# A gated sum of a Fourier mix and a SwiGLU layer on one core: gate applied at the spill, two Strassen sums left to DMA, w2 parts in the common buffer pool, wider x blocks

## The chip, the core and the metric

The kernel runs on one core of one Trainium2 chip. The metric is the device time of one execution in microseconds; every time given for the runs is the median of three. Engine names are those of the profile: PE is TensorE's matmul, PEld its weight load, DVE is VectorE, ACT is ScalarE, POOL is GpSimd, SP is SyncE, which here only issues DMAs. A name with a q (SPq, ACTq, POOLq) is the engine's instruction queue.

## The reference

With x of 2048 rows and 512 columns, in float32:

```python
g = sigmoid((x * gate_w).sum(-1, keepdims=True))           # one gate per row
a = Cr_seq @ (x @ Cr_hid.T) - Ci_seq @ (x @ Ci_hid.T)      # real part of a 2-D Fourier transform
b = (silu(x @ w1) * (x @ w3)) @ w2                         # F = 1376
out = g * a + (1 - g) * b
```

The Fourier matrices are inputs, 2048 x 2048 and 512 x 512, real and imaginary parts.

## The kernel before

Every product of float32 matrices is made of three matmuls: `split(hi, lo, src)` (L75) rounds `src` to the faster type on ScalarE (`hi`, L76) and takes the rest on VectorE (`lo`, L77), and `mm3` (L79) multiplies hi by hi, hi by lo and lo by hi. All matmuls therefore stand at L81, all splits at L76 and L77. On top of that the products are made in blocks of two by two by a scheme with seven products in place of eight (Strassen's in Winograd's form). It needs sums of blocks: T1 = B12 + B11, T2 = T1 + B22, T3 = B22 + B12, T4 = T2 + B21 (in the gate and up products the signs differ).

The work runs in five stages on PE. Everything is computed transposed: features on the 128 partitions, rows of x along the free axis.

1. **Gate and up, first half of x** (`gate_up(1, 11)`, product 0 being made without the scheme by `plain`). Each of 11 steps i makes 128 columns of both w1 and w3 for 1024 rows of x: `first1`, `first2` and `second`. The x blocks are loaded by `load_xo` as two tiles of 512 columns for each block, summed by `sum_xo` (L144) and split by `split_xo`. A score column for the gate g is part of the last w1 block; `put_score` brings it out. The result h(i) (128 x 1024) lies in a buffer of the pool `f4` until it is used.
2. **Down projection, first half** (`down(0)`): 11 chunks c of 24 matmuls in eight accumulators `acc`. `prep_dn` splits h(c) into `ho` (two buffers in the pool `dn`) and w2's part into `w2o` (two buffers in `dn`), and writes the split part of w2 to memory (`w2sp`). At the end b times (1 - g) is stored in `nbsp`. `gates` makes the sigmoid and stores it in `gsp`.
3. **Gate and up, second half of x** (`gate_up(11, 22)`). Beside it `prep_d` splits the Fourier matrix along D and stores it (`dsp`).
4. **Down projection, second half** (`down(1)`). The split w2 parts come back from `w2sp`, by a DMA that ScalarE issues (L260) into `w2o`. Beside it `load_a` loads x once more in another layout (xr) and makes and splits its sums (xm) into A1 and A2, and the first blocks of the sequence matrix (`cc`, tiles c) are loaded.
5. **The Fourier transform** (matmuls into P). First along the sequence: four blocks `blk` 0 to 3 of 28 steps, weights A1 and A2; then along D: blocks 4 and 5 of 14 steps, weights D1 and D2. Each step is 12 matmuls; the last two steps are made together, 24 matmuls for each half of the rows. `load_c` issues loads eight steps ahead of a step, `sum_c` makes T1, T2 and T4 on VectorE four steps ahead (L509), `split_c` splits three steps ahead into one of four `zo` buffers. T3 is made in the buffer of B22 by an accumulating DMA that GpSimd issues once B22 has been split (L520). The four results Z of a block of the sequence transform are written to `zsp` by `spill`, and the D transform loads its blocks from there. `spill` of the D transform multiplies by the gate (L561), adds b's part (L566, at the end L563) and stores the output.

The pool `f4` has 13 buffers of 128 x 1024 float32. h, x staging, w2's raw parts, xr, xm, gates, c blocks and output parts all take their buffers there, and an instruction that needs one waits until one is released.

The framework orders each engine's instructions by program order and by its own estimate of when each is ready, so an instruction can stand some steps ahead of its place in the text; each engine then works through its list in order. A DMA waits in its issuing queue, and what is behind it waits too. The order of steps and the lead of loads in the transform are written out by hand:

```python
CHAIN = (("P1", "B11"), ("P5", "T1"), ("P6", "T2"), ("P3", "B22"),
         ("P7", "T3"), ("P2", "B21"), ("P4", "T4"))
ORDER = [CHAIN] * NTB + [tuple(CHAIN[i] for i in (0, 5, 1, 2, 3, 4, 6))] * (NTB // 2)
LEAD = 3
AHEAD = 5
```

## Time and profile before

| | |
|---|---|
| three runs | 736.51, 736.87, 739.08 us; median 736.87 us |
| the profiled execution | 742.17 us, of which the span is 740.3 us |
| granted TensorE clock, mean | 0.994 |
| PE busy | 724.2 us, 98% of the span, 3145 matmuls |
| VectorE busy | 537.8 us, 73% |
| ScalarE busy | 362.4 us, 49% |
| GpSimd busy | 17.8 us, 2% |
| DMA | 128.21 MB, 173 GB/s on average |

The profile is one execution on the chip. Its stages can be told by the tiles that the matmuls write: C, X, Y and Z for gate and up, acc for the down projection, P for the Fourier transform. Matmuls are pipelined, so a busy PE is not PE at its peak: the pace (matmuls in a stretch against its length) says more. A wait is put down to the engine or DMA whose signal came last by this profile. "Granted clock" is the share of TensorE's full clock in a stretch.

### The profile page before, as it was taken

The numbers are of one execution on the slowest core, as the hardware profiler recorded it, in microseconds if no ns is written. First come the engines' busy times: TensorE is split into PE (matmuls) and PEld (weight loads), VectorE is DVE, ScalarE is ACT, GpSimd is POOL, SyncE is SP. The second block draws the span as 40 slices with busy tenths as digits, with TensorE's granted clock in tenths as the row PEclk, the third lists the DMA queues.
The fourth block names the chain that finished last, engine by engine and source line by source line (L and its number), as shares of the span: only waits on it lengthen the run. The fifth ranks groups of instructions, "written<-read, shape, count | busy, mean of one in ns | idle before, by whom it ended". The sixth has DMA issues, their size and how long they took to land.

```text
span 740.3 us, 8392 instructions
## 1 busy us (share of the span) xinstructions
PE 724.2 (98%) x3145; PEld 592.2 (80%) x3145; DVE 537.8 (73%) x681; ACT 362.4 (49%) x476; POOL 17.8 (2%) x24
## 2 busy tenths in 40 slices
PE   8999999999999999889999999999999999999996
PEld 5888878888888888778888888888888888887784
DVE  5997786584598968596857686667657675565977
ACT  5755565453466645461444445444444543453532
POOL 0000000000000000000010001000100010000000
PEclk9999999999999999999999999999999999999999
DMA  7122135835157305693767724783378329997642
GB/s 255 35 81 85 58 122 191 283 129 200 58 205 264 128 0 159 232 300 141 277 107 235 256 86 87 226 260 110 65 221 270 128 41 269 395 345 213 215 109 90
DMA packets 37324, 128.21 MB, mean 173 GB/s; under 512 B 3874, under 2 KB 4002, under 8 KB 36260
## 3 DMA queue, kind: packets, MB, share of 16 engines
q1 hardware_dynamic: 32532, 110.91, 43.1%
q0 software_dynamic: 2880, 10.49, 7.9%
q10 hardware_dynamic: 1872, 6.29, 2.6%
q8 instruction: 24, 0.39, 0.2%
q14 instruction: 16, 0.13, 0.1%
HBM read 96.73 MB, written 30.94 MB: 172 GB/s over the span
## 4 chain that ended last, share of the span: by engine, by line
PE 83%; issue 5%; DVE 5%; DMA 5%; ACT 1%; SPq 0%; ACTq 0%; POOLq 0%; POOL 0%; DVEq 0%
PE P L81 42%; PE X L81 15%; PE acc L81 13%; PE Z L81 8%; PE Y L81 4%; DMA c<-zsp 2%; PE C L81 2%; DMA xs<-xt 1%; DMA w2o<-w2sp 1%; DVE zo L77 1%; DVE xs L144 1%; DVE c L509 0%; DVE xo L77 0%; DVE ho L77 0%; DVE w2o L77 0%
## 5 line engine op out<-in xcount | busy, mean ns | idle before, releaser
L81 PE MATMUL P<-zo,a 128*128 128x512 f32 x1344 | 304.8, 389 | 0.0
L81 PEld LDWEIGHTS P<-zo,a 128*128 128x128 f32 x1344 | 252.3, 188 | 52.3
L77 DVE TENSOR_TENSOR zo<-c,zo 128x1024 fp32r<-128x1024 f32 x140 | 171.1, 1224 | 105.3 <-ACT zo L76 103.4
L76 ACT ACTIVATE zo<-c 128x1024 fp32r<-128x1024 f32 x140 | 147.6, 1059 | 177.8 <-PE P L81 142.7
L81 PE MATMUL acc<-ho,w2o 128*128 128x512 f32 x528 | 124.2, 397 | 4.2 <-DMA w2o<-w2sp 2.1
L81 PEld LDWEIGHTS acc<-ho,w2o 128*128 128x128 f32 x528 | 101.1, 192 | 27.0 <-ACT ho L76 2.5
L81 PE MATMUL X<-xo,wb 128*128 128x512 f32 x378 | 94.2, 390 | 0.2
L81 PEld LDWEIGHTS X<-xo,wb 128*128 128x128 f32 x378 | 70.6, 188 | 16.3 <-ACT u L239 0.8
L509 DVE TENSOR_TENSOR c<-c,c 128x1024 f32<-128x1024 f32 x60 | 73.3, 1224 | 10.5 <-DMA c<-cc 6.7
L81 PE MATMUL P<-zo,d 128*128 128x512 f32 x336 | 78.2, 392 | 2.6 <-DVE zo L77 1.3
L81 PEld LDWEIGHTS P<-zo,d 128*128 128x128 f32 x336 | 62.8, 188 | 17.8 <-DVE zo L77 2.6
L81 PE MATMUL X<-xo,wa 128*128 128x512 f32 x126 | 32.9, 391 | 0.0
L81 PE MATMUL Y<-xo,wa 128*128 128x512 f32 x126 | 32.3, 389 | 0.0
L81 PE MATMUL Z<-xo,wa 128*128 128x512 f32 x126 | 32.2, 389 | 0.0
L81 PE MATMUL Z<-xo,wb 128*128 128x512 f32 x126 | 32.2, 389 | 0.0
L77 DVE TENSOR_TENSOR wb<-wu,wb 128x1024 fp32r<-128x1024 f32 x21 | 25.7, 1224 | 8.5 <-ACT wb L76 8.2
L77 DVE TENSOR_TENSOR ho<-h,ho 128x1024 fp32r<-128x1024 f32 x22 | 26.9, 1221 | 6.9 <-ACT ho L76 6.9
L76 ACT ACTIVATE wa<-ws 128x768 fp32r<-128x768 f32 (+2 forms) x23 | 18.8, 816 | 25.2 <-PE Z L81 25.2
L76 ACT ACTIVATE ho<-h 128x1024 fp32r<-128x1024 f32 x22 | 23.1, 1050 | 11.2 <-PE acc L81 9.9
L520 POOL DMA_DIRECT2D c<-cc x16 | 14.1, 879 | 599.6 <-DVE zo L77 599.6
L81 PEld LDWEIGHTS X<-xo,wa 128*128 128x128 f32 x126 | 23.4, 188 | 5.4 <-DVE wa L77 0.4
L81 PEld LDWEIGHTS Z<-xo,wa 128*128 128x128 f32 x126 | 23.6, 188 | 5.0 <-ACT u L241 0.2
(92 smaller groups left out, 538.7 us busy)
## 6 DMA issues: line engine op xcount, KB each, us to landing
c<-cc SPq DMA_DIRECT2D x64, 512.0 KB, 4.4
ws<-w SPq DMA_DIRECT2D x21, 512.0 KB, 3.6
c<-cc POOLq DMA_DIRECT2D x16, 512.0 KB, 5.4
c<-zsp SPq DMA_DIRECT2D x16, 512.0 KB, 8.1
w2sp<-w2o SPq DMA_DIRECT2D x11, 512.0 KB, 2.7
w2o<-w2sp ACTq DMA_DIRECT2D x11, 512.0 KB, 4.5
nbsp<-b SPq DMA_DIRECT2D x8, 512.0 KB, 3.1
dsp<-d SPq DMA_DIRECT2D x4, 1024.0 KB, 5.7
```

Of the source, the lines that this page charges most:

```text
L76: nc.scalar.activation(hi, src, AF.Copy)
L77: nc.vector.tensor_sub(lo, src, hi.bitcast(F32))
L81: nc.tensor.matmul(ps, u, v, start=first and n == 0, stop=last and n == 2, skip_group_check=chain)
L144: nc.vector.tensor_sub(staged(g, q, k), *(staged(g, q, v) for v in SUMS[k]))
L509: nc.vector.tensor_add(t, t, RAW[blk, b, q])
L520: nc.gpsimd.dma_start(src, block(blk, 1, q), accum_op=ALU.add)
```

## The change

- **Gate.** In the sequence transform each result Z is multiplied by the gate of its columns before it is stored (two multiplications of 128 x 512 for each of 16 results; for the result of P4 these read the accumulator, in place of two ScalarE copies). The gate of a block is loaded when the block begins, into a tile of its own with two buffers. The D transform no longer multiplies; its last result is added straight from the accumulator. The two gate tiles beside D1 and D2 and their loads are gone.
- **T1 and T3 of the D transform.** Both get a buffer of their own: B12 is loaded into it and B11 or B22 is added by an accumulating DMA of GpSimd, right after the load. T1's load has its place two steps before the block's first step, T3's at its fifth step, less the lead of eight steps. T2 and T4 are still summed on VectorE, in T1's buffer. The sequence transform keeps its way.
- **w2 parts.** In the second down projection the split parts go to buffers of `f4` and are loaded by SP, two chunks ahead.
- **x blocks.** One tile of 128 x 1024 for each block and each sum in place of two of 512 wide, each in a buffer taken when it is loaded or summed; one DMA, one sum and one split for each (the first split stays in two halves). The split blocks lie in one tile. The first w block is issued ahead of the first x block, and SP issues all of them.
- **Warm-up.** 11 matmuls on zeros at the start in place of 7.

The core of the diff (the host's arrangement of x, and the same renaming in `prod`, `plain` and x1 to x3, are left out):

```diff
-WARM = 7
+WARM = 11
...
+    def load_xo(g, k):
+        if g not in XO:
+            XO[g] = xo.tile([P, 2, 7, 2, 512], F32R, tag="xo", name=f"xo{g}")
+        ST[g, k] = wide(f"xs{g}_{k}")
+        nc.sync.dma_start(ST[g, k], xt[g, XRAW.index(k)])
...
     def sum_xo(g, k):
-        for q in range(2):
-            nc.vector.tensor_sub(staged(g, q, k), *(staged(g, q, v) for v in SUMS[k]))
+        ST[g, k] = wide(f"xs{g}_{k}")
+        nc.vector.tensor_sub(ST[g, k], *(ST[g, v] for v in SUMS[k]))
...
+    def load_w2(i):
+        if NC <= i < 2 * NC:
+            W2O[i] = f4.tile([P, 2, 512], F32R, tag="f4", name=f"w2o{i}")
+            nc.sync.dma_start(W2O[i].bitcast(F32), w2sp[i - NC])
...
     def prep_dn(i):
         g, c = divmod(i, NC)
-        o = dn.tile([P, 2, 512], F32R, tag="w2o", name=f"w2o{i}")
-        if g == 1:
-            nc.scalar.dma_start(o.bitcast(F32), w2sp[c])
-        elif c % 2 == 0:
+        if g == 0 and c % 2 == 0:
...
     def down(g, extra):
...
         for c in range(NC):
+            if c == 0:
+                load_w2(g * NC + 1)
+            load_w2(g * NC + c + 2 if g == 1 else 0)
             if c + 1 < NC:
                 prep_dn(g * NC + c + 1)
...
                 if i == i1 - 2:
+                    load_w2(i1 - NC)
                     prep_dn(i1 - NC)
...
-    load_xo(0, 0, 1, (nc.sync, nc.scalar))
     load_w(0, 0, 1)
+    load_xo(0, "B11")
...
+    NEED = [(("B11", 0, 0), ("B12", 1, 1), ("B22", 2, 1), ("B21", 5, 0))] * NTB + [
+        (("B11", 0, 0), ("B21", 1, 0), ("T1", 2, 6), ("B22", 3, 1), ("T3", 5, 6))] * (NTB // 2)
...
     def split_c(m):
...
-        if form == "B22":
-            nc.gpsimd.dma_start(src, block(blk, 1, q), accum_op=ALU.add)
+        if form == "B22" and blk < NTB:
+            nc.gpsimd.dma_start(src, block(blk, "B12", q), accum_op=ALU.add)

     def load_c(m):
         while LOADS and LOADS[0][0] <= m:
             _, blk, k, q = LOADS.pop(0)
-            r = RAW[blk, BLOCKS[k], q] = wide(f"c{k}_{blk}_{q}")
-            nc.sync.dma_start(r, block(blk, k, q))
+            r = RAW[blk, k, q] = wide(f"{k}_{blk}_{q}")
+            nc.sync.dma_start(r, block(blk, "B12" if k in ("T1", "T3") else k, q))
+            if k in ("T1", "T3"):
+                nc.gpsimd.dma_start(r, block(blk, "B11" if k == "T1" else "B22", q),
+                                    accum_op=ALU.add)
...
     def spill(blk, k, t, ps=None):
-        last = blk == len(NQ) - 1 and k == 1
+        src = [t[:, r] for r in range(2)] if ps is None else ps
         if blk < NTB:
-            if ps is not None:
-                for r in range(2):
-                    nc.scalar.activation(t[:, r], ps[r], AF.Copy)
+            for r in range(2):
+                nc.vector.tensor_mul(t[:, r], src[r], GT[blk])
             return nc.sync.dma_start(z_rows(blk, k), flat(t))
-        gt, b, o = gated.pop((blk, k))
+        b, o = other.pop((blk, k))
+        if ps is None:
+            nc.vector.tensor_add(flat(t), flat(t), flat(b))
+            return nc.sync.dma_start(o, t)
         for r in range(2):
-            nc.vector.tensor_mul(t[:, r], t[:, r] if ps is None else ps[r], gt)
-            if last:
-                nc.vector.tensor_add(t[:, r], t[:, r], b[:, r])
-                (nc.scalar if r else nc.sync).dma_start(o[:, r], t[:, r])
-        if not last:
-            nc.vector.tensor_add(flat(t), flat(t), flat(b))
-            nc.sync.dma_start(o, t)
+            nc.vector.tensor_add(t[:, r], ps[r], b[:, r])
+            (nc.scalar if r else nc.sync).dma_start(o[:, r], t[:, r])
...
+    def load_gate(blk):
+        GT[blk] = ut.tile([P, 512], F32, tag="gate", name=f"gate{blk}", bufs=2)
+        nc.sync.dma_start(GT[blk], gsp[blk // 2, :, blk % 2 * 512 : (blk % 2 + 1) * 512])
...
     def step(m):
         blk, q, k, form = STEPS[m]
+        if m == START[blk] and blk < NTB:
+            load_gate(blk)
...
-    GT = [yd.tile([P, 1024], F32, tag=f"g{g}", name=f"g{g}") for g in range(2)]
...
-        elif k < 2 * KD + 2:
-            nc.sync.dma_start(GT[k - 2 * KD], gsp[k - 2 * KD])
```

More of the change, by code (lines that the diff above doesn't have):

```diff
@@ L64, in fnet_swiglu_gate_kernel @@
     dn_cm, dn = pool("dn", 2, "right")
-    xo_cm, xo = pool("xo", 2, "left")
+    xo_cm, xo = pool("xo", 1, "left")
     wo_cm, wo = pool("wo", 2, "left")
@@ L121, in fnet_swiglu_gate_kernel, with flat_x, split_xo @@
     XO, ST = {}, {}
-    def load_xo(g, t, j, queues=(nc.sync, nc.sync)):
-        if g not in ST:
-            ST[g] = [[wide(f"xs{g}_{q}_{i}") for i in range(4)] for q in range(2)]
-            XO[g] = [xo.tile([P, 2, 7, 512], F32R, tag="xo", name=f"xo{g}_{q}") for q in range(2)]
-        for q in range(2):
-            queues[q].dma_start(ST[g][q][t][:, j * 512 : (j + 1) * 512],
-                                xt[g, q, :, t * 1024 + j * 512 : t * 1024 + (j + 1) * 512])
-    AT = {"B12": (0, 0), "B11": (0, 1), "B21": (1, 0), "B22": (1, 1),
-          "T1": (2, 0), "T2": (2, 1), "T3": (3, 0), "T4": (3, 1)}
+    XRAW = ("B12", "B11", "B21", "B22")
+    def flat_x(ap):
+        return ap.rearrange("p q n -> p (q n)")
+    def load_xo(g, k):
[3 more added lines that the diff above has]
+        nc.sync.dma_start(ST[g, k], xt[g, XRAW.index(k)])
     OPS = ("B11", "B21", "B22", "T1", "T2", "T3", "T4")
     SUMS = {"T1": ("B12", "B11"), "T2": ("B22", "T1"), "T3": ("B22", "B12"), "T4": ("B21", "T2")}
-    def staged(g, q, k):
-        t, j = AT[k]
-        return ST[g][q][t][:, j * 512 : (j + 1) * 512]
     def sum_xo(g, k):
-        for q in range(2):
-            nc.vector.tensor_sub(staged(g, q, k), *(staged(g, q, v) for v in SUMS[k]))
-    def split_xo(g, *ks):
-        n = OPS.index(ks[0])
-        for q in range(2):
-            o, (t, j) = XO[g][q], AT[ks[0]]
-            split(o[:, 0, n : n + len(ks), :].rearrange("p a n -> p (a n)"),
-                  o[:, 1, n : n + len(ks), :].rearrange("p a n -> p (a n)"),
-                  ST[g][q][t][:, j * 512 : (j + len(ks)) * 512])
+        ST[g, k] = wide(f"xs{g}_{k}")
+        nc.vector.tensor_sub(ST[g, k], *(ST[g, v] for v in SUMS[k]))
+    def split_xo(g, k):
+        o = XO[g][:, :, OPS.index(k)]
+        split(flat_x(o[:, 0]), flat_x(o[:, 1]), ST[g, k])
     WS, WA, WB = {}, {}, {}
@@ L191, in prod @@
         w, wi = (WA[i], wi) if wi < 3 else (WB[i], wi - 3)
+        x = XO[g]
         for q in range(2):
             sl = slice(q * P, (q + 1) * P)
-            x = XO[g][q]
-            mm3(ps, w[:, 0, wi, sl], w[:, 1, wi, sl], x[:, 0, xi, :], x[:, 1, xi, :],
+            mm3(ps, w[:, 0, wi, sl], w[:, 1, wi, sl], x[:, 0, xi, q, :], x[:, 1, xi, q, :],
                 start and q == 0, q == 1, chain)
@@ L266, in prep_dn @@
         if g == 0:
+            o = dn.tile([P, 2, 512], F32R, tag="w2o", name=f"w2o{i}")
             split(o[:, 0], o[:, 1], W2R[g, c // 2][:, (c % 2) * 512 : (c % 2 + 1) * 512])
             nc.sync.dma_start(w2sp[c], o.bitcast(F32))
-        W2O[i] = o
+            W2O[i] = o
         t = dn.tile([P, 2, 1024], F32R, tag="ho", name=f"ho{i}")
@@ L356, in xb @@
         def xb(k):
-            return lambda q, h: XO[0][q][:, h, k, :]
+            return lambda q, h: XO[0][:, h, k, q, :]
         w21 = lambda h, sl: a21[:, h, sl]
@@ L378, in fnet_swiglu_gate_kernel @@
     load_w(0, 1, 4)
-    load_xo(0, 1, 0)
-    load_xo(0, 0, 0)
+    load_xo(0, "B21")
+    load_xo(0, "B12")
     load_w(1)
-    load_xo(0, 1, 1)
+    load_xo(0, "B22")
     load_w(2)
@@ L389, in fnet_swiglu_gate_kernel @@
     prep_wa(0, 0, 1)
-    split_xo(0, "B11")
+    for q in range(2):
+        split(XO[0][:, 0, 0, q], XO[0][:, 1, 0, q], ST[0, "B11"][:, q * 512 : (q + 1) * 512])
     next(step)
@@ L396, in fnet_swiglu_gate_kernel @@
     next(step)
-    for q in range(2):
-        sl = slice(q * 512, (q + 1) * 512)
-        split(b12[:, 0, sl], b12[:, 1, sl], staged(0, q, "B12"))
+    split(b12[:, 0], b12[:, 1], ST[0, "B12"])
     next(step)
@@ L425, in x1 @@
     def x1():
-        for t, j in ((0, 1), (1, 0), (0, 0), (1, 1)):
-            load_xo(1, t, j)
+        for k in ("B11", "B21", "B12", "B22"):
+            load_xo(1, k)
     def x2():
@@ L433, in x2 @@
         sum_xo(1, "T2")
-        split_xo(1, "T1", "T2")
+        split_xo(1, "T1")
+        split_xo(1, "T2")
     def x3():
@@ L438, in x3 @@
         sum_xo(1, "T4")
-        split_xo(1, "T3", "T4")
+        split_xo(1, "T3")
+        split_xo(1, "T4")
         split_xo(1, "B22")
@@ L481, in fnet_swiglu_gate_kernel @@
     START = [sum(NQ[:blk]) * len(CHAIN) for blk in range(len(NQ) + 1)]
-    BLOCKS = ("B11", "B12", "B22", "B21")
+    NEED = [(("B11", 0, 0), ("B12", 1, 1), ("B22", 2, 1), ("B21", 5, 0))] * NTB + [
+        (("B11", 0, 0), ("B21", 1, 0), ("T1", 2, 6), ("B22", 3, 1), ("T3", 5, 6))] * (NTB // 2)
+    PLACE = [{"T1": "B12", "T2": "B12", "T4": "B12", "T3": "B22"}] * NTB + [
+        {"T2": "T1", "T4": "T1"}] * (NTB // 2)
     LEAD = 3
@@ L488, in fnet_swiglu_gate_kernel @@
     LOADS = sorted((START[blk] + n * nq - e + q, blk, k, q)
-                   for blk, nq in enumerate(NQ) for q in range(nq)
-                   for k, n, e in (((0, 0, 0), (1, 1, 1), (2, 2, 1), (3, 5, 0)) if blk < NTB else
-                                   ((0, 0, 0), (3, 1, 0), (1, 2, 1), (2, 3, 1))))
+                   for blk, nq in enumerate(NQ) for q in range(nq) for k, n, e in NEED[blk])
     def z_rows(tb, k):
@@ L497, in block @@
         if blk < NTB:
-            return cc[blk, k, q]
-        return z_rows(2 * (blk - NTB) + (0, 1, 1, 0)[k], (0, 0, 2, 2)[k] + q)
+            return cc[blk, ("B11", "B12", "B22", "B21").index(k), q]
+        return z_rows(2 * (blk - NTB) + (k in ("B12", "B22")), 2 * (k in ("B21", "B22")) + q)
     def sum_c(m):
@@ L506, in sum_c @@
         b = {"T1": "B11", "T2": "B22", "T4": "B21"}.get(form)
-        if b:
-            t = RAW[blk, "B12", q]
+        if b and form in PLACE[blk]:
+            t = RAW[blk, PLACE[blk][form], q]
             nc.vector.tensor_add(t, t, RAW[blk, b, q])
@@ L515, in split_c @@
         blk, q, k, form = STEPS[m]
-        src = RAW[blk, {"T1": "B12", "T2": "B12", "T4": "B12", "T3": "B22"}.get(form, form), q]
+        src = RAW[blk, PLACE[blk].get(form, form), q]
         t = ZO[m] = zo.tile([P, 2, 1024], F32R, tag="zo", name=f"zo{m}")
         split(t[:, 0], t[:, 1], src)
-        if form == "B22":
-            nc.gpsimd.dma_start(src, block(blk, 1, q), accum_op=ALU.add)
+        if form == "B22" and blk < NTB:
+            nc.gpsimd.dma_start(src, block(blk, "B12", q), accum_op=ALU.add)
     def load_c(m):
@@ L551, in spill @@
     def spill(blk, k, t, ps=None):
-        last = blk == len(NQ) - 1 and k == 1
+        src = [t[:, r] for r in range(2)] if ps is None else ps
         if blk < NTB:
-            if ps is not None:
-                for r in range(2):
-                    nc.scalar.activation(t[:, r], ps[r], AF.Copy)
+            for r in range(2):
+                nc.vector.tensor_mul(t[:, r], src[r], GT[blk])
             return nc.sync.dma_start(z_rows(blk, k), flat(t))
-        gt, b, o = gated.pop((blk, k))
+        b, o = other.pop((blk, k))
+        if ps is None:
+            nc.vector.tensor_add(flat(t), flat(t), flat(b))
+            return nc.sync.dma_start(o, t)
         for r in range(2):
-            nc.vector.tensor_mul(t[:, r], t[:, r] if ps is None else ps[r], gt)
-            if last:
-                nc.vector.tensor_add(t[:, r], t[:, r], b[:, r])
-                (nc.scalar if r else nc.sync).dma_start(o[:, r], t[:, r])
-        if not last:
-            nc.vector.tensor_add(flat(t), flat(t), flat(b))
-            nc.sync.dma_start(o, t)
-    gated, LAST = {}, []
+            nc.vector.tensor_add(t[:, r], ps[r], b[:, r])
+            (nc.scalar if r else nc.sync).dma_start(o[:, r], t[:, r])
+    GT, other, LAST = {}, {}, []
+    def load_gate(blk):
+        GT[blk] = ut.tile([P, 512], F32, tag="gate", name=f"gate{blk}", bufs=2)
+        nc.sync.dma_start(GT[blk], gsp[blk // 2, :, blk % 2 * 512 : (blk % 2 + 1) * 512])
     def load_nb(blk, k):
@@ L579, in load_nb @@
         nc.sync.dma_start(b, nb)
-        gated[blk, k] = GT[tb // 2][:, tb % 2 * 512 : (tb % 2 + 1) * 512], b, o
+        other[blk, k] = b, o
     def step(m):
         blk, q, k, form = STEPS[m]
+        if m == START[blk] and blk < NTB:
+            load_gate(blk)
         if q == 0 and blk >= NTB and k in RESULT:
@@ L681 @@
     xb = [xh[:, :, 0, 1], xh[:, :, 0, 0], xh[:, :, 1, 0], xh[:, :, 1, 1]]
-    xq = x.T.reshape(2, 2, P, 2, 2, TB).transpose(3, 1, 2, 0, 4, 5)
-    xq = xq.transpose(0, 1, 3, 4, 2, 5)
+    xq = x.T.reshape(2, 2, P, 2, 2, TB).transpose(3, 0, 4, 2, 1, 5)
+    xq = [xq[:, 0, 1], xq[:, 0, 0], xq[:, 1, 0], xq[:, 1, 1]]
     w13 = np.zeros((2, D, NC * P), np.float32)
@@ L695 @@
         "xn": np.stack(xb, 2).reshape(NG, P, 2 * D),
-        "xt": np.stack([xq[:, :, 0, 1], xq[:, :, 0, 0], xq[:, :, 1, 0], xq[:, :, 1, 1]], 3)
-        .reshape(2, 2, P, 4 * TB),
+        "xt": np.stack(xq, 1).reshape(2, 4, P, 2 * TB),
         "cc": np.stack(cb, 1).reshape(NTB, 4, NG // 2, P, 2 * TB),
```

## The prediction

> **What bounds the kernel now.** I read the page first, then a table of stages, then the chain of waits, then the waits and timelines of the stages that lose time. The page:

> ```profile
> span 740.3 us, 8392 instructions
> PE 724.2 (98%) x3145; PEld 592.2 (80%) x3145; DVE 537.8 (73%) x681; ACT 362.4 (49%) x476; POOL 17.8 (2%) x24
> ```

> TensorE is the bound, and only time in which it is held up can be won. No matmul is added or removed. The chain of waits, in order of time, gives the pace and the places:

> ```profile
> 281.07 16.47 PE acc L81 x72
> 299.52 23.63 PE acc L81 x96
> 323.17 7.39 DMA w2o<-w2sp
> 330.69 18.19 PE acc L81 x72
> 348.89 310.11 PE P L81 x1368
> ```

> The last row is the pace: 310.11/1368 = 0.2267 us a matmul, with nothing lost in 310 us. The down projection of the second half (281.07 to 348.89, 67.8 us) has 264 matmuls, 59.8 us at that pace: 8.0 us are lost there. The stage table says how (columns: busy PE, PEld, DVE, ACT, POOL; granted clock; DMA share; GB/s):

> ```profile
> 176.00:281.00 105.00, 105.00 (x463) 86.27 (x462) 80.05 (x138) 58.11 (x91) 0.00 (x0) 1.00 0.39 135
> 281.00:300.00 19.00, 17.03 (x75) 13.65 (x74) 14.91 (x30) 13.77 (x22) 0.00 (x0) 1.00 0.59 192
> 300.00:324.00 24.00, 24.00 (x100) 19.66 (x99) 18.46 (x36) 11.02 (x19) 0.00 (x0) 0.93 0.82 274
> 324.00:349.00 25.00, 22.88 (x95) 18.44 (x94) 19.67 (x26) 9.98 (x15) 0.00 (x0) 0.93 0.49 165
> 349.00:450.00 101.00, 101.00 (x447) 83.67 (x446) 71.24 (x63) 46.74 (x52) 3.62 (x4) 1.00 0.60 187
> ```

> PE stands still about 2 us twice (19.00-17.03, 25.00-22.88), and after each halt the granted clock is 0.93 for some 25 us, 1.7 us lost each time: 2 x (2.1+1.7) = 7.6 of the 8.0. The timelines name the first halt:

> ```profile
> 292.03 0.33 ACTq L260 DMA_DIRECT2D w2o<-w2sp  x1
> 298.47 1.04 ACT L76 ACTIVATE ho<-h 128x1024 fp32r<-128x1024 f32 x1
> 299.50 1.94 PE L81 MATMUL acc<-ho,w2o 128*128 128x512 f32 x6 [1.97 <-ACT ho L76]
> DMA to landing us min/median/max: 3.1/4.5/7.4
> ```

> PE starts at 299.50, before the split named (298.47+1.04 = 299.51) has ended, so the name is wrong: the w2 load issued at 292.03 plus the longest landing of that tile (last line, the view of tile w2o) is 299.4. The second halt is the w2 load issued at 323.17 and landed 7.39 us later. Both were issued when a chunk (24 matmuls, 5.44 us) freed one of two buffers, so they had 5.44 us and took 7.4.

> The second transform has 336 matmuls (76.2 us) and takes from 653.4 to 734.1: 4.4 us lost, here:

> ```profile
> 681.91 0.50 PE L81 MATMUL P<-zo,d 128*128 128x512 f32 x1 [1.18 <-ACT zu L617]
> 682.69 3.07 PE L81 MATMUL P<-zo,d 128*128 128x512 f32 x12 [0.28 <-DVE zo L77]
> 686.53 36.02 PE L81 MATMUL P<-zo,d 128*128 128x512 f32 x156 [0.76 <-DVE zo L77]
> 722.83 11.29 PE L81 MATMUL P<-zo,d 128*128 128x512 f32 x47 [0.28 <-DVE zo L77]
> ```

> These are T3's steps (the 11th and 12th of 14 in each block, so 27 us after 653.4 and again). T3's sum is an accumulating DMA on GpSimd's queue, issued only after B22 was split:

> ```profile
> 670.43 0.86 POOL L520 DMA_DIRECT2D c<-zsp  x1 [56.29 <-DVE zo L77]
> 673.84 0.86 POOL L520 DMA_DIRECT2D c<-zsp  x1 [2.55 <-DMA c<-zsp]
> ```

> Last, the tail. The last matmul ends at 734.12, then VectorE still multiplies by the gate and adds, and the store goes out:

> ```profile
> 735.73 0.69 DVE L561 TENSOR_TENSOR zc<-P,g 128x512 f32<-128x512 f32 x1
> 736.45 0.69 DVE L563 TENSOR_TENSOR zc<-zc,nb 128x512 f32<-128x512 f32 x1
> ```

> **Gate moved to the spill: the tail.** In the second transform 16 multiplications of 0.64 us (a pair takes 1.29) leave VectorE. In the last 14 us six of them go, so VectorE is no longer behind: the last add can start at 734.15, when PE is done, and ends at 734.84 instead of 737.14. That is -2.3 us; nothing else ends later, the store's 3.2 us stay. In the first transform 32 multiplications come in (20.6 us) and 8 ScalarE copies of 0.60 go. VectorE there goes from 203.3 of 304 us to 223.9, 74%. The page shows the splits of zo waiting 103.4 us for ScalarE, and those 142.7 us for PE's buffers, so a split starts 8.2 us (three steps of 2.72) before its matmul and needs 2.3; where a sum and a split share a step (2.45 of 2.72 us), a pair of 1.29 fits in the 5.9 us left. Cost nothing; with that cover gone, 1.29 us at each of 16 results would be 20.6. The spill's store on SP is issued 1.3 us later; behind it stand c loads, ordered eight steps (21.8 us) ahead against a landing of 4.4 to 8.1. The gate loads are as many bytes as before, in four parts.

> **T1 and T3 by DMA on loads.** T3's load and accumulation move from two steps to six products ahead, so those 4.4 us should go; I take all. Four 1.22 us sums leave VectorE, which is busy 31.68 of 32 us between 685 and 717. Added are four loads and four accumulations. From the page's queue shares: the plain queue takes 0.431 x 740.3/110.91 = 2.88 us of all engines a MB, 1.5 us a load; the accumulating one 0.079 x 740.3/20 = 2.9 us each. Together 17.7 us of DMA over some 100 us whose share is 0.58. Between 624 and 663 the DMA engines are full, with the 7 MB of D parts; two T1 accumulations there (5.8 us) push loads back, while two gate loads (3 us) go. Bounds 0 to +3 us at the transform's opening; I take +0.3, because in the trace a T1 sum of this block ran already at 625.8, 28 us early.

> **w2 parts in pool tiles.** Loads go out two chunks ahead (10.9 us against a worst landing of 7.4) on SP, so both halts and their slow clock go: -8.0. ScalarE loses 11 issues of 0.33. The price is buffers: the pool of 13 holds the nine unsplit h parts at chunk 0 and falling by one per chunk, so 4+c were free for x parts, sums and c blocks; three w2 parts leave 1+c. The first x part then finds one buffer and its sums none until w2 part 0 is released at 286.5, against 282.96 before: VectorE starts forms 4 us later and the next ones wait for buffers in turn. Eight forms at 3.6 us from start to start and nine h splits at 1.14 are 39 us of the 59.8, so all is ready by the end; but a form that waits for its x part on VectorE or ScalarE holds the h split queued behind it, for which PE then waits. That gives 0 to two halts of 3.8; I take +2.5, under one halt, since only chunks 1 to 3 are short.

> **x blocks 1024 wide, 11 warm matmuls.** A split goes from 2 x 0.69 to 1.22 us on VectorE and 2 x 0.62 to 1.06 on ScalarE, but its first half is ready 0.45 to 0.5 later. Four more warm matmuls at 0.43 end at 6.1, just before PE's first real one at 6.22. The first x block is issued second on SP, 0.46 later, while its w part is ready earlier. Net 0; bounds +0.6 (a first half late) and -1.7 below.

> [...]

> **Sum.** -2.3 -4.4 +0.3 -8.0 +2.5 +0 = -11.9 on the profiled execution's 742.17 (740.3 span and 1.87 around it): 730.3. The median of the runs is 736.87, 5.3 lower. If they have all the halts, the result is 725.0; if what they lack is these halts, 730.3. The trace cannot say which; the runs differ by 2.6 us among themselves, about one halt with its slow clock, so some have one and some not. I lean to the second: **729**.

> **Rivals.** (1) The w2 halts stay: the loads stand on SP behind x loads that wait for buffers. For it: SP waits 113.9 us in five waits for buffers of c loads. Against: two chunks of lead. Then 742.17-2.3-4.4 = 735.5, in the runs 730.2 to 735.5. [...] (2) Slower: buffer hunger in the down projection. If h splits are held behind starved forms in five chunks, at 3.8 each, that is +19 against -14.7: 746.5, in the runs about 741; it decides from the fourth halt on. For it: 1+c free buffers. Against: VectorE has 20 us to spare. (3) The sums by DMA do not come early: SP is held at stores (zsp at 633.7 and 643.5), and accumulations land late again: the 4.4 stays, 734.7, in the runs 729.4 to 734.7.

> **Numbers.** Forecast 0.55, rival 1 0.2, rival 2 0.1, rival 3 0.1, a faster start 0.05. About 0.5% (3.7 us) is what a measurement can tell: faster is below 733.2, slower above 740.6. Faster 0.51+0.1+0.05+0.04 = 0.70; same 0.19; slower 0.11. The range reaches from 723.5 (all halts gone in the runs and the clock's 1.7) to 739 (rival 2 with three halts).

> **What would show it.** Right: no PE wait for w2o, granted clock 1.00 from 281 to 349, the P stage starting 5 us or more earlier; no PE wait in the T3 steps; the last add ending 0.7 us after the last matmul. Wrong: PE waits for ho in chunks 1 to 5 with forms ahead of it on VectorE; SP waiting long at w2o; PE waiting for zo at P1 or P2 of the second transform, or in the first one.

## The result and the profile after

The changed kernel takes 728.69 us (median of four runs, 728.55 to 729.82), the kernel before on the same chip 736.69. The ratio is 0.9888, 95% interval 0.9865 to 0.9911: faster by 1.1%, 8.0 us. The prediction said 729.0. The total was right. Two of its terms were not, the w2 parts and the start, and that their errors hardly show in the total is in part luck, as told below.

The page after and its chain of waits (longest pieces, in order of time):

```profile
span 727.0 us, 8380 instructions
PE 719.2 (99%) x3149; PEld 589.6 (81%) x3149; DVE 542.6 (75%) x676; ACT 358.5 (49%) x458; POOL 21.2 (3%) x28
```

```profile
114.51 59.88 PE acc L81 x264
...
279.58 21.82 PE acc L81 x96
307.23 5.35 DMA w2o<-w2sp
312.71 11.18 PE acc L81 x48
342.15 381.11 PE P L81 x1680
```

The last row is the whole Fourier transform, both parts, without a gap: 381.11/1680 = 0.2268 us a matmul. A w2 load is still in the chain. The table of stages over much the same places as before (busy PE, PEld, DVE, ACT, POOL; granted clock; DMA share; GB/s):

```profile
174.00:279.00 105.00, 105.00 (x463) 86.22 (x462) 79.98 (x139) 58.06 (x91) 0.00 (x0) 1.00 0.38 135
279.00:300.00 21.00, 21.00 (x94) 17.38 (x93) 13.86 (x27) 9.80 (x16) 0.00 (x0) 1.00 0.53 185
300.00:320.00 20.00, 19.55 (x87) 15.88 (x86) 14.19 (x27) 12.59 (x18) 0.00 (x0) 1.00 0.66 252
320.00:342.00 22.00, 20.44 (x90) 16.31 (x88) 21.94 (x33) 13.86 (x21) 0.00 (x0) 1.00 0.67 240
342.00:646.00 304.00, 303.85 (x1340) 251.71 (x1341) 222.56 (x214) 135.17 (x144) 15.79 (x18) 1.00 0.64 200
646.00:723.30 77.30, 77.25 (x341) 63.65 (x339) 57.23 (x56) 35.33 (x41) 5.25 (x6) 1.00 0.73 240
```

No stretch has a slow clock; the second down projection loses 0.45 and 1.56 us of PE in two stretches and the transforms almost nothing. The tail of VectorE, from its timeline:

```profile
720.88 0.68 DVE L571 TENSOR_TENSOR zc<-P,nb 128x512 f32<-128x512 f32 x1
723.29 0.69 DVE L571 TENSOR_TENSOR zc<-P,nb 128x512 f32<-128x512 f32 x1 [1.72 <-PE P L81]
```

VectorE now waits 1.72 us for the last matmul (end 723.25) and finishes at 723.98.

Stage lengths in us, from the start of one stage's first matmul to that of the next (tail: from the last matmul's end to the end of the span). The second column is a second trace of the kernel before, told of below:

| | before, first trace | before, second trace | after |
|---|---|---|---|
| to the first product | 6.22 | 6.77 | 6.22 |
| first gate and up | 109.28 | 108.91 | 108.12 |
| first down projection | 60.26 | 60.34 | 59.88 |
| second gate and up | 105.16 | 105.21 | 105.19 |
| second down projection | 67.81 | 62.85 | 62.74 |
| sequence transform | 304.65 | 304.65 | 304.78 |
| D transform | 80.75 | 80.32 | 76.32 |
| tail | 6.14 | 6.19 | 3.76 |
| span | 740.3 | 735.2 | 727.0 |

Against the first trace 13.3 us went, against the second 8.2: the difference is the second down projection of the kernel before, and the 8.2 are what the runs show.

### The profile page after: what moved, and what is told of

Same layout as the page of the kernel before. It is cut to its first block, busy times and chain, and to the rows that moved or that the text cites. A ratio compares the mean times of both kernels' runs of the same rounds, so it can differ in the third digit from the quotient of the medians.

```text
span 727.0 us, 8380 instructions
## 1 busy us (share of the span) xinstructions
PE 719.2 (99%) x3149; PEld 589.6 (81%) x3149; DVE 542.6 (75%) x676; ACT 358.5 (49%) x458; POOL 21.2 (3%) x28
## 4 chain that ended last, share of the span: by engine, by line
PE 94%; DVE 2%; ACT 2%; DMA 1%; issue 1%; SPq 0%; ACTq 0%
PE P L81 52%; PE X L81 16%; PE acc L81 13%; PE Z L81 8%; PE Y L81 4%; PE C L81 2%; DMA w2o<-w2sp 1%; DMA xs_B<-xt 1%; DVE ho L77 0%; DVE zo L77 0%; ACT zo L76 0%; ACT a L76 0%; DVE xm L103 0%; ACT L303 0%; ACT ho L76 0%
## 5 line engine op out<-in xcount | busy, mean ns | idle before, releaser
L81 PE MATMUL P<-zo,a 128*128 128x512 f32 x1344 | 304.9, 389 | 0.7 <-DVE b L290 0.7
L81 PEld LDWEIGHTS P<-zo,a 128*128 128x128 f32 x1344 | 252.3, 188 | 53.4 <-DVE b L290 1.1
L76 ACT ACTIVATE zo<-B 128x1024 fp32r<-128x1024 f32 x124 | 131.3, 1060 | 161.0 <-PE P L81 147.1
L77 DVE TENSOR_TENSOR zo<-B,zo 128x1024 fp32r<-128x1024 f32 x124 | 151.2, 1223 | 74.9 <-ACT zo L76 74.3
L81 PE MATMUL acc<-ho,w2o 128*128 128x512 f32 x528 | 120.6, 390 | 1.5 <-DMA w2o<-w2sp 1.5
L81 PEld LDWEIGHTS acc<-ho,w2o 128*128 128x128 f32 x528 | 99.0, 188 | 22.8 <-issue 1.4
L81 PE MATMUL X<-xo,wb 128*128 128x512 f32 x378 | 94.3, 391 | 0.2
L81 PEld LDWEIGHTS X<-xo,wb 128*128 128x128 f32 x378 | 70.5, 188 | 16.3 <-DVE u L235 0.6
L81 PE MATMUL P<-zo,d 128*128 128x512 f32 x336 | 76.3, 389 | 0.0
L81 PEld LDWEIGHTS P<-zo,d 128*128 128x128 f32 x336 | 63.1, 188 | 13.1
L511 DVE TENSOR_TENSOR B<-B,B 128x1024 f32<-128x1024 f32 x48 | 58.5, 1223 | 7.3 <-DMA B<-cc 5.3
L77 DVE TENSOR_TENSOR ho<-h,ho 128x1024 fp32r<-128x1024 f32 x22 | 26.9, 1221 | 10.4 <-ACT ho L76 10.4
L81 PE MATMUL X<-xo,wa 128*128 128x512 f32 x126 | 33.1, 391 | 0.0
L81 PE MATMUL Z<-xo,wb 128*128 128x512 f32 x126 | 32.3, 389 | 0.0
L77 DVE TENSOR_TENSOR wb<-wu,wb 128x1024 fp32r<-128x1024 f32 x21 | 25.7, 1224 | 8.6 <-ACT wb L76 8.3
L81 PE MATMUL Y<-xo,wa 128*128 128x512 f32 x126 | 32.1, 389 | 0.0
L76 ACT ACTIVATE wa<-ws 128x768 fp32r<-128x768 f32 (+2 forms) x23 | 18.8, 816 | 27.0 <-PE Z L81 25.5
L81 PE MATMUL Z<-xo,wa 128*128 128x512 f32 x126 | 32.0, 389 | 0.0
L522 POOL DMA_DIRECT2D B<-cc x16 | 14.1, 878 | 545.9 <-DVE zo L77 545.8
L77 DVE TENSOR_TENSOR zo<-T,zo 128x1024 fp32r<-128x1024 f32 x16 | 19.6, 1223 | 12.4 <-ACT zo L76 12.4
L81 PEld LDWEIGHTS X<-xo,wa 128*128 128x128 f32 x126 | 23.5, 188 | 5.4 <-DVE wa L77 0.6
L76 ACT ACTIVATE ho<-h 128x1024 fp32r<-128x1024 f32 x22 | 23.2, 1053 | 9.3 <-PE acc L81 7.9
```

Source lines behind the costliest of these rows:

```text
L76: nc.scalar.activation(hi, src, AF.Copy)
L77: nc.vector.tensor_sub(lo, src, hi.bitcast(F32))
L81: nc.tensor.matmul(ps, u, v, start=first and n == 0, stop=last and n == 2, skip_group_check=chain)
L511: nc.vector.tensor_add(t, t, RAW[blk, b, q])
L522: nc.gpsimd.dma_start(src, block(blk, "B12", q), accum_op=ALU.add)
```

## The experiments

All kernels of one group ran on one chip with the kernel before. The kernel before varies from run to run and from chip to chip (median 740.47 beside the first group, 738.26 the second, 737.57 the third), the changed kernel, run on two chips, hardly (728.69 and 729.20), so kernels are compared with the changed kernel by their times and by the stages of their traces. A trace is one execution of each.

**The changed kernel once more.**

> The changed kernel once more, as the yardstick for the three kernels beside it on the same chip. Expected 728.7 us, ratio to the kernel before 0.989; the down projection of the second half 62.6 us, the D transform 76.3 us with no wait of PE.

It took 729.20 us, ratio 0.9859 (0.9834 to 0.9884); second down projection 63.37, D transform 76.32, tail 3.77. This is the yardstick.

**w2 parts back in two buffers of their own, issued by ScalarE.**

```diff
-        if NC <= i < 2 * NC:
+        if False:
             W2O[i] = f4.tile([P, 2, 512], F32R, tag="f4", name=f"w2o{i}")
             nc.sync.dma_start(W2O[i].bitcast(F32), w2sp[i - NC])
...
+        o = dn.tile([P, 2, 512], F32R, tag="w2o", name=f"w2o{i}")
+        if g == 1:
+            nc.scalar.dma_start(o.bitcast(F32), w2sp[c])
```

> The changed kernel with the w2 parts back in two buffers of dn, loaded by ScalarE when a chunk frees one. Theory (the lead of two chunks removed the halts): PE waits for w2o again, the down projection of the second half takes 66 to 68 us in place of 62.6, and the time rises by 3 to 5 us to 732 to 734. Rival (the halts of the kernel before were of that one execution and rare): the stage stays at 62 to 63 us or gets shorter, since its buffers are no longer short, and the time is 727 to 729.

It took 727.96 us, ratio 0.9839 (0.9811 to 0.9866): 1.2 less than the yardstick, not 3 to 5 more. The intervals of the two ratios overlap, but four of its five runs lie below every run of the yardstick. PE halts at w2 parts as in the kernel before, here in the trace of its slowest run (729.66):

```profile
297.13 16.60 PE L81 MATMUL acc<-ho,w2o 128*128 128x512 f32 x72 [1.33 <-DMA w2o<-w2sp]
315.27 11.17 PE L81 MATMUL acc<-ho,w2o 128*128 128x512 f32 x48 [1.54 <-ACT ho L76]
```

The second halt is put down to ScalarE's split of ho, but the split for this chunk had ended on both engines by 312.19; the w2 part, issued at 308.33, is what is left. The halts are shorter than the 2.1 of the first trace and no slow clock follows; the stage takes 63.86. So the rival's time held, though not its picture and, in this trace, not its 62 to 63 us: the halts are there, but two buffers with one chunk of lead lose no more, by the times, than three from the common pool with two.

**T1 and T3 of the D transform as before.**

```diff
-        (("B11", 0, 0), ("B21", 1, 0), ("T1", 2, 6), ("B22", 3, 1), ("T3", 5, 6))] * (NTB // 2)
+        (("B11", 0, 0), ("B21", 1, 0), ("B12", 2, 1), ("B22", 3, 1))] * (NTB // 2)
...
-        if form == "B22" and blk < NTB:
+        if form == "B22":
```

> The changed kernel with T1 of the D transform summed on VectorE again and T3 added by DMA only after B22 has been split; all else as changed. Theory (the late accumulation made PE wait in T3's steps): the D transform takes 79 to 81 us in place of 76.3, with waits of PE in the 11th and 12th step of a block, time 731 to 733. Rival (VectorE, full with gate multiplications, made it late; these are gone here): the D transform stays under 77.5 us, time 729 to 730.

It took 731.27 us, ratio 0.9885 (0.9862 to 0.9908), 2.1 over the yardstick; D transform 77.75, tail 4.03. PE waits at T3 in the first block only:

```profile
675.03 0.50 PE L81 MATMUL P<-zo,d 128*128 128x512 f32 x1 [0.54 <-ACT zu L625]
675.81 49.07 PE L81 MATMUL P<-zo,d 128*128 128x512 f32 x215 [0.27 <-DVE zo L77]
```

Between the two expectations: with the multiplications off VectorE, T1 on VectorE and the late accumulation of T3 together cost 1.43 in the stage, not 4.4. GpSimd's queue shows where the multiplications had come in. The accumulations of the second block, first in the kernel before, then here:

```profile
714.77 0.89 POOL L520 DMA_DIRECT2D c<-zsp  x1 [40.07 <-DVE zo L77]
717.04 0.87 POOL L520 DMA_DIRECT2D c<-zsp  x1 [1.38 <-DVE zo L77]
```

```profile
703.63 0.89 POOL L521 DMA_DIRECT2D B<-zsp  x1 [35.24 <-DVE zo L77]
706.37 0.88 POOL L521 DMA_DIRECT2D B<-zsp  x1 [1.85 <-DVE zo L77]
```

Counted from the first matmul of the block (694.60 and 686.64) they are issued 20.2 and 22.4 us in, and here 17.0 and 19.7: without the multiplications VectorE reaches the split of B22 about 3 us sooner, and PE no longer waits. In the first block both kernels issue them 17 and 20.4 us in, and there PE still waits.

**The gate at the output as before.**

```diff
-            for r in range(2):
-                nc.vector.tensor_mul(t[:, r], src[r], GT[blk])
+            if ps is not None:
+                for r in range(2):
+                    nc.scalar.activation(t[:, r], ps[r], AF.Copy)
...
+            nc.vector.tensor_mul(t[:, r], t[:, r] if ps is None else ps[r], gt)
```

> The changed kernel with the gate applied in the D transform again (two gate tiles of 1024 loaded beside D1 and D2, two multiplications at each output, none at the spill). Theory (only the tail gains): from the last matmul's end to the end of the span 6.0 to 6.3 us in place of 3.75, no new wait of PE, time 2.0 to 2.6 us longer, 730.7 to 731.3. Rival (VectorE in the D transform is relieved enough to matter to PE too): the D transform itself also gets 1 to 3 us longer, time 732 to 734.

It took 730.10 us, ratio 0.9871 (0.9847 to 0.9896), 0.9 over the yardstick; the D transform stays at 76.32, the tail is 4.82. No wait of PE in the D transform, as the theory said, but less than half of the tail:

```profile
723.62 0.69 DVE L569 TENSOR_TENSOR zc<-P,g 128x512 f32<-128x512 f32 x1
724.35 0.69 DVE L571 TENSOR_TENSOR zc<-zc,nb 128x512 f32<-128x512 f32 x1
```

VectorE takes up the last product as soon as PE is done (723.58), where in the kernel before it was 1.6 us late (735.73 after 734.12). Whether T1's sums, gone from VectorE, or the earlier T3 did this is not told apart.

**Both undone.** The two edits above together.

> The changed kernel with both the gate and the sums T1 and T3 of the D transform as they were before; the w2 parts, the x blocks and the warm-up stay as changed. Undone alone, T1 and T3 cost 1.7 us in the traces (D transform 77.75 in place of 76.32, tail 4.03 in place of 3.77) and the gate 1.05 us (tail 4.82). Theory (the two overlap: VectorE's multiplications and the late T3 make each other worse, so together they cost more than the sum): D transform 80 to 81 us, tail 6.1, time 734 to 736, 5 to 7 us over the changed kernel. Rival (the costs add up): 2.8 us, 732.

It took 735.48 us, ratio 0.9965 (0.9954 to 0.9976), 6.3 over the yardstick: D transform 79.72, tail 6.18. The costs do not add up (2.1 + 0.9 = 3.0); half of the loss is that each makes the other worse. The traces say the same: 5.8 us in D transform and tail, against 1.7 and 1.1 alone. PE and, at the end, VectorE, from the timelines:

```profile
678.38 0.49 PE L81 MATMUL P<-zo,d 128*128 128x512 f32 x1 [1.01 <-ACT zo L76]
679.63 35.81 PE L81 MATMUL P<-zo,d 128*128 128x512 f32 x156 [0.76 <-DVE zo L77]
715.73 11.28 PE L81 MATMUL P<-zo,d 128*128 128x512 f32 x47 [0.28 <-DVE zo L77]
```

```profile
728.65 0.68 DVE L568 TENSOR_TENSOR zc<-P,g 128x512 f32<-128x512 f32 x1
729.37 0.69 DVE L570 TENSOR_TENSOR zc<-zc,nb 128x512 f32<-128x512 f32 x1
```

This is the picture of the kernel before, T3's waits in both blocks and the last add 3.0 us after the last matmul (727.0).

**A second trace of the kernel before.**

> The kernel before, unchanged, for a second trace. Its runs reach from 736 to 742 us. Theory (the two halts at w2o parts are there in every execution, and whether the slow clock of 3.4 us follows each is a matter of how long the halt is and where it falls): two halts of 1.5 to 2.5 us at w2o in the down projection of the second half, at the same chunks, with zero to two stretches at half clock, so that stage 63.5 to 68 us; the D transform 80 to 81 us and the tail 6.1 us as in the first trace. Rival (the halts come and go): none, or at other chunks.

It took 737.26 us (span 735.2). The halts are at the same tile, shorter, and the clock stays up:

```profile
298.71 27.65 PE L81 MATMUL acc<-ho,w2o 128*128 128x512 f32 x120 [0.61 <-DMA w2o<-w2sp]
327.69 16.57 PE L81 MATMUL acc<-ho,w2o 128*128 128x512 f32 x72 [1.32 <-DMA w2o<-w2sp]
```

The stage takes 62.85 us, 5 less than in the first trace, below the 63.5 to 68 expected and no more than in the changed kernel. That is nearly all of the 5.3 us by which the profiled execution was above the median. The granted clock of other runs bears this out: one stretch of 3.41 us at half clock takes 0.0023 from its mean, the first trace with two has 0.994, this one with none 0.999. Of the 43 runs of the kernel before beside the three groups, 25 show 0.998 or 0.999, as without such a stretch, 13 show 0.996 or less, as with at least one, and two of these 0.994. The halts themselves are at the start of chunks 3 and 8 in both traces.

**7 warm-up matmuls in the changed kernel.**

> The changed kernel with 7 warm-up matmuls in place of 11. Theory (the clock opens after a stretch of continuous work; with 7 matmuls PE stands idle from 4.4 us to its first real matmul near 6): the first half's gate and up takes 0.8 to 1.5 us longer, 109 to 109.6 in place of 108.1, and the time rises by about 1 us to 730. Rival (the start is paced by the splits, not by the clock): no change within 0.3 us, 729.2.

It took 730.66 us, ratio 0.9898 (0.9882 to 0.9914), 1.5 to 2.0 over the changed kernel; the first gate and up takes 109.84 us (109 to 109.6 expected) and ends at 115.59 in place of 114.34. The two timelines, first with 7, then with 11, where VectorE's split of B21 is shown too:

```profile
5.75 3.22 PE L81 MATMUL C<-xo,wa 128*128 128x512 f32 x6 [1.39 <-ACT xo L76]
8.77 2.40 PE L81 MATMUL C<-xo,a 128*128 128x512 f32 x6
11.01 2.92 PE L81 MATMUL C<-xo,wa 128*128 128x512 f32 x12
```

```profile
6.22 0.49 PE L81 MATMUL C<-xo,wa 128*128 128x512 f32 x1 [0.32 <-ACT xo L76]
6.95 1.42 PE L81 MATMUL C<-xo,wa 128*128 128x512 f32 x5 [0.23 <-DVE xo L77]
8.21 1.56 PE L81 MATMUL C<-xo,a 128*128 128x512 f32 x6
8.87 1.22 DVE L77 TENSOR_TENSOR xo<-xs_B,xo 128x1024 fp32r<-128x1024 f32 x1 [0.43 <-ACT xo L76]
9.61 3.11 PE L81 MATMUL C<-xo,wa 128*128 128x512 f32 x12
```

The first twelve matmuls take 5.26 us with 7 (11.01-5.75) and 3.39 with 11 (9.61-6.22). The trace's clock records put the full clock at 10.64 and at 5.62 us. In the three traces of kernels with 7 it came between 10.2 and 10.6 us, in the ten with 11 between 4.6 and 7.0. The theory's stretch of continuous work, as measured: with 7 the full clock came 4.89 us after PE began its real matmuls at 5.75 (in the first trace of the kernel before 4.28 after 6.22, at 10.50), with 11 4.43 us after the warm-up began at 1.19.

**11 warm-up matmuls in the kernel before.**

> The kernel before with 11 warm-up matmuls in place of 7. In the changed kernel 4 fewer cost 1.7 us in the first gate and up, and the clock opened at 10.6 us in place of 4.6 to 7.0. Theory (the warm-up alone is what the start gains): the first gate and up takes 107.6 to 108.4 us in place of 108.9 to 109.3, the clock opens before 7.1 us, time 1.2 to 1.8 us under the kernel before. Rival (with x in two loads of 512 the start is paced by loads and splits): less than 0.5 us.

It took 736.02 us beside 737.57, ratio 0.9970 (0.9951 to 0.9990); full clock at 5.22, to the end of the first gate and up 113.98 in place of 115.50 and 115.68. So the warm-up alone makes what the start gains. The first down projection takes 60.59 here, with narrow x blocks, and 59.88 in every trace with wide ones. The second down projection, whose w2 parts are as before, takes 64.39 in this trace, with halts of 1.22 and 1.84 us and the clock up: a third measure of what these halts cost, between the other two.

**w2 parts one chunk ahead, in the common pool.**

```diff
-            load_w2(g * NC + c + 2 if g == 1 else 0)
+            if c:
+                load_w2(g * NC + c + 1 if g == 1 else 0)
```

> The changed kernel with w2 parts loaded one chunk ahead in place of two, still by SP and into the common pool. Theory (the lead is what can hide a landing of 3 to 7 us, and SP's queue eats it): PE waits for w2o in more chunks, the down projection of the second half takes 65 to 70 us, time 732 to 737. Rival (the third buffer taken from the pool costs as much as the lead brings): 62 to 63.5 us, 728 to 729.

It took 731.68 us, ratio 0.9913 (0.9891 to 0.9935), 2.5 over the yardstick; second down projection 67.27, with halts of 2.57 and 2.14 us and one stretch of slow clock, in its slowest run (732.98). So the lead of two chunks is needed on SP; moved there without it, the loads fare worse than on ScalarE (727.96).

**The store of the gate on ScalarE.** What is left of the halts in the changed kernel can be read in SP's own timeline. Chunk 6 began at 312.71 us after a halt of 0.45:

```profile
306.33 0.32 SPq L306 DMA_DIRECT2D gsp<-gt  x1
306.76 0.37 SPq L466 DMA_DIRECT2D xr<-xn  x1
307.23 0.72 SPq L251 DMA_DIRECT2D w2o<-w2sp  x1
```

The store had to wait for the sigmoid, and the w2 part of chunk 6, issued behind it at 307.23, landed 5.35 us later, at 312.6, in time with the end of that halt.

```diff
-        nc.sync.dma_start(gsp[g], t)
+        nc.scalar.dma_start(gsp[g], t)
```

> The changed kernel with only the store of the gate (gsp) issued by ScalarE; w2 loads as changed. Both moves together took the down projection of the second half to 59.88 us, the pace itself, and the time to 725.75. Theory (each move removes its own halt): the halt of 0.6 to 0.9 us at chunk 6 goes, that of 1.2 to 2.0 at the last chunks and the wait at the first transform step stay, stage 61.5 to 62.3 us, time 727 to 728. Rival (the store alone set off all of it, by making everything behind it late): stage 60 us, time 726.

It took 728.34 us, ratio 0.9868 (0.9843 to 0.9894), 0.4 to 0.9 under the changed kernel; stage 62.47. Time and stage lie just above the theory's ranges, but its picture holds: the halt at chunk 6 is gone, the later two stay:

```profile
299.69 34.39 PE L81 MATMUL acc<-ho,w2o 128*128 128x512 f32 x151
335.66 5.73 PE L81 MATMUL acc<-ho,w2o 128*128 128x512 f32 x24 [1.58 <-DMA w2o<-w2sp]
341.94 3.28 PE L81 MATMUL P<-zo,a 128*128 128x512 f32 x13 [0.56 <-DVE b L290]
```

**The same, and the last two w2 parts one chunk earlier.** This kernel ran before the one above. The last part was issued at 329.87 in the changed kernel (329.66 in the run above), behind c loads that waited for buffers.

```diff
-            load_w2(g * NC + c + 2 if g == 1 else 0)
+            load_w2(g * NC + c + 2 if g == 1 and c < 7 else 0)
+            if g == 1 and c == 6:
+                load_w2(g * NC + 9)
+            if g == 1 and c == 7:
+                load_w2(g * NC + 10)
```

> The changed kernel with two moves: the store of the gate (gsp) is issued by ScalarE, which has just made it, in place of SP; and the w2 parts of the last two chunks are loaded one chunk earlier, in chunks 6 and 7. Theory (what is left of the halts comes from SP's queue: the store waited on SP until 306.33 with the w2 part of chunk 6 behind it, and the last w2 part was issued at 329.87 behind loads that waited for buffers): no wait for w2o, down projection of the second half 60.0 to 61.0 us in place of 63.0, time 726.5 to 727.5. Rival (buffers, not the queue, are short): the halts move to other chunks and the time stays at 729.

It took 725.75 us (725.46 to 725.81), ratio 0.9829 (0.9814 to 0.9844): faster than both kernels. The stage runs at the pace:

```profile
279.28 60.04 PE L81 MATMUL acc<-ho,w2o 128*128 128x512 f32 x264
339.16 6.07 PE L81 MATMUL P<-zo,a 128*128 128x512 f32 x26
```

All w2 halts are gone, and with them the wait for VectorE's `b` at the first transform step. Stage and time came out a little below the theory's ranges. Most of the gain is that of the two advanced loads, 2.6 of the 2.9 to 3.5 us against the changed kernel.

## Why the prediction was right, and where not

- **Gate at the spill, -2.3: right as a size.** The tail went from 6.14 to 3.76. The attribution was too simple: undone alone the gate costs 1.06 of the tail and T1 and T3 0.26; the rest of the 2.4 comes only of both. VectorE in the sequence transform is busy 222.56 of 304 us (223.9 forecast), and the stage grew by 0.13 us.
- **T1 and T3, -4.4 + 0.3: the size right, the cause half.** The D transform lost 4.43 (4.0 against the second trace), and nothing was paid at its opening. T3's accumulations of the first block are issued 2.3 and 4.9 us into the stage in place of 17.1 and 20.5, so the early T3 came about as forecast. But undone alone these sums cost 1.43 of it. The step that failed is that the 4.4 us were put down to the late T3 alone and the tail to the gate alone: VectorE, 31.68 of 32 us busy there, took part in both losses, so they were one term of 5.8 us (D transform and tail in `undo_both` against the changed kernel: 3.40 + 2.42). The sum of the two sizes came out right because both edits were made.
- **w2 parts, -8.0 + 2.5: wrong.** The step that failed is that two chunks of lead would end the halts, worth 8.0. The 8.0 was read from one execution, in which two stretches of slow clock followed the halts; the two other traces with these loads on ScalarE lose 3.0 and 4.6 in this stage (62.85 and 64.39 against 59.8), and the changed kernel still loses 2.9, halts of 0.45 and 1.02 us at w2 parts among it, where the prediction had named no such wait as a sign of being right. By `undo_w2` the gain of the move is nil, or a loss of 1. The price of +2.5 was about the size of the loss that came (2.9), by luck, for the mechanism was not the one told: VectorE did start its forms 4.4 us later (287.33 against 282.96) and PE waited for no h split; PE waited for w2 parts on SP, rival 1's picture, and 0.7 us for VectorE's `b` at the stage's end.
- **Warm-up and x blocks, 0: wrong by 1.6 to 2.** No run that the prediction had shows the 1.7 that its bound and its range take off for a faster start; in its place the runs showed a gain of 1.55 us in the kernel before, 1.5 to 2.0 in the changed one. The wide split of B21 did not hold the faster matmuls up: it ended at 10.09, but PE could begin that block at 9.61 with the high half. The wide x blocks gave 0.4 to 0.7 in the first down projection, which was not forecast; that it was they is shown by elimination, since that stage stays at 59.88 with each of the other edits undone.
- **From the profiled execution to the runs: right, but leant to and not shown.** The prediction said that the trace could not tell whether the runs have these halts, and leaned to the answer that they lack them. The second trace has them short and without slow clock: 62.85 us in place of 67.81. So the wrongly priced w2 gain was largely taken out again in the step from the profile to the runs. What the forecast took off beyond that (729.0 in place of 730.3) happens to stand in for the gain of 1.6 or more at the start that it lacked. That is luck: of the 8.2 us between the second trace and the changed kernel, 6.4 are the D transform and the tail, 0.1 the second down projection, and 1.8 the stages up to the end of the first down projection, for which the forecast had nothing. The ends of the range were not worked out alike: 725.0 less 1.7 is 723.3, not 723.5, and 739 is three halts on the profiled execution (738.9), which in the runs would be 733.6.
- **Rivals.** Rival 1's mechanism was there without its size; rivals 2 and 3 did not occur. By `undo_w2` the move to SP gained nothing by itself. But with one chunk of lead the same loads took 731.68 us on SP and 727.96 on ScalarE (where they have buffers of their own), and moving one store to ScalarE ended a halt of 0.45: more than an issue of 0.33. So here not only the time of issuing counted, but also what stood ahead in the queue of the engine that issued.

## What to carry to other kernels

Before a stall in one trace is priced, take a second trace of the same kernel, above all if the profiled time stands off the median: of the 8 us seen here 5 were gone in a second trace and 3.4 in a third. Edits that relieve the same full engine can be one term, not several, and are told apart only by undoing each and both. A load moved to a shared in-order queue was only as early as the wait in front of it (here a w2 part went out at 307.23, behind a store that waited until 306.33): read that queue's own timeline for stores that wait for results; moving one such store and advancing two loads won 3 us more than the change did with its w2 part, most of it by the two loads.

## What the runs showed of the hardware

In these traces the length of a halt alone does not tell whether a slow clock follows it. Stages of the kernel before, first trace, and of the kernel with w2 parts one chunk ahead:

```profile
297.30:300.60 3.30, 1.33 (x7) 0.95 (x6) 1.36 (x2) 2.40 (x4) 0.00 (x0) 1.00 0.60 216
300.70:304.00 3.30, 3.30 (x9) 2.53 (x9) 2.35 (x7) 0.00 (x0) 0.00 (x0) 0.50 1.00 319
```

```profile
306.00:309.50 3.50, 0.93 (x5) 0.50 (x4) 1.61 (x5) 1.31 (x3) 0.00 (x0) 1.00 1.02 400
309.50:313.00 3.50, 3.50 (x17) 2.89 (x16) 3.50 (x9) 2.96 (x5) 0.00 (x0) 1.00 0.90 335
331.20:334.50 3.30, 1.16 (x6) 0.68 (x5) 3.30 (x8) 2.22 (x4) 0.00 (x0) 1.00 0.70 259
334.70:338.00 3.30, 3.30 (x9) 2.61 (x8) 3.30 (x4) 0.73 (x1) 0.00 (x0) 0.50 0.82 276
```
